# Weight blocks cast by DMAs that GpSimd issues, the scale applied to y instead of w_in, a written-out order for group 1, and four output buffers

## The chip, the cores and the metric

The kernel runs on one core of a Trainium2 chip. The metric is device time of one execution in microseconds, lower is better. A core has TensorE (PE, matmuls into PSUM), VectorE (DVE), ScalarE (ACT), GpSimd (POOL) and SyncE (SP), each with a queue of its own that it works through in order, and 16 DMA engines that all queues share. DMAs are issued by SP (the profile calls their queue q1, hardware_dynamic) or by POOL (q0, software_dynamic).

## The reference

Two parts, the first feeding the second. Shapes: q, k, v and f_logit are (4, 8, 768, 48), w_in is 384 x 2048, w_out is 2048 x 384, all float32.

```python
f = 1.0 / (1.0 + np.exp(-f_logit))
for t in range(S):                                   # per batch and head, state is 48 x 48
    state = f[:, :, t, :, None] * state + np.einsum('bhd,bhe->bhde', k[:, :, t], v[:, :, t])
    y[:, :, t] = np.einsum('bhd,bhde->bhe', q[:, :, t], state)
x = y.transpose(0, 2, 1, 3).reshape(B * S, H * D)    # 3072 x 384
h = x @ w_in
P = a[0] + a[1] * h + a[2] * h**2 + a[3] * h**3
Q = 1.0 + np.abs(b[0]) * np.abs(h) + np.abs(b[1]) * h**2
out = (P / (Q + 1e-06)) @ w_out
```

## The kernel before

**Tiling.** The sequence is cut in 6 chunks of 128 positions. In the recurrent part a unit n is one chunk for two of the four batches, so there are 12 units; in the dense part a group n is one chunk (all four batches, 512 rows) and 512 of the 2048 hidden columns, so there are 24 groups, four to a chunk. Unit 2c and 2c+1 give the input xT of chunk c, which groups 4c to 4c+3 read.

**A unit** is built by functions named a_: `a_ef` (ACT, two activations of the forget logits fn, L110 and L111), `a_cs` (PE, cumulative sum, L117), `a_exp` twice (ACT, tiles A, L124), `a_mul` (DVE, qn and kn times A into qkp, L130 and L131), `a_T` and `a_Te` (PE transposes L139, ACT evacuation L147), `a_sc` twice (PE scores, L181), `a_mask` twice (DVE, scm, L190), `a_sv`, `a_al`, `a_st` (the state: PE, ACT, DVE L234), `a_y` and `a_ye` (PE L201, ACT evacuation ysb L217), `a_x` and `a_xe` (PE transposes L242, ACT xT L250).

**A group** is built by functions named m_: `m_h` twice (PE, half a group each, L263), `m_y` (ACT, hy, L271), `m_sq` and `m_abs` (DVE, h2 shown as h L277, z L282), `m_p1` (DVE, tile t, L326 and L327), `m_p2` (pb, L332), `m_p3` (L336), `m_u` and `m_ln` twice (PE L291, ACT lq L313), `m_ex` (ACT qi, L320), `m_g` (DVE gall, L343). `m_o` and `m_oe` are the output product (PE L360) and its evacuation to osb with a DMA to HBM (ACT L368 or DVE L366, SP L369); they run for the chunk before.

**Order.** The pools are rings, but the order of the instructions on each engine is that of the source (`manual_schedule`). A prologue from L383 to L515 takes units 0 to 2 and groups 0 and 1 as far as L336; `busy(k)` in it are k matmuls on zeros. Then one loop over n takes group n further together with the unit that is due, with a branch for odd and one for even n, and conditions for n == 1. A last part handles chunk 5 without units.

**Loads.** `load(n)` issues two DMAs each for fn, kn and qn on SP (192 KB each, in pieces of 192 bytes) and two for vn on POOL, which cast float32 to bfloat16 on the way; the ld pool holds three units. Weights come in eight blocks of 768 KB: `load_w_in(g)` and `load_w_out(g)` issue a DMA on SP into one of two float32 staging buffers (wst), and POOL casts the block to bfloat16. For w_in POOL also multiplies by `sig[:, 0:1]`, one number that depends on b alone (`coefficients()` computes it), because the dense part works on a scaled h. Group g of chunk 0 needs block g of w_in; the w_out blocks are first read by `m_o` in iteration n = 5.

**Output tail.** The last chunk's four products use three PSUM tiles: b = 0 and 1 share the tile `op2`, b = 2 has `opl`, b = 3 has `op`. osb has two buffers (pool ms).

## Time and profile before

| | us |
|---|---|
| median of 3 runs | 285.42 |
| the 3 runs | 284.39, 285.42, 287.75 |
| profiled execution | 285.07 |
| its span, first to last instruction | 283.2 |
| its mean granted TensorE clock | 0.958 |

The profiled execution lies 0.35 us under the median, and 1.87 us of its time lie outside the span. In the profile's rows the first number is the start and the second the duration in us; brackets at the end of a row tell how long the engine sat idle before it and what ended the wait. A row of several instructions has their count as x2.

### The profile page before, as it was taken

How to read it: one execution, taken by the hardware profiler on the slowest of the kernel's cores; microseconds unless marked ns; L12 is line 12 of the kernel's file. 1: busy time of each engine (PE TensorE's matmuls, PEld its weight loads, DVE VectorE, ACT ScalarE, POOL GpSimd, SP SyncE). 2: the span in 40 equal slices, each digit the busy share in tenths (PEclk: the TensorE clock that was granted, in tenths of full speed). 3: DMA queues.
4: the chain of work that ended last, by engine and by line, in shares of the span. 5: the costliest groups of instructions: out<-in, count | busy, mean ns of one | idle time of the engine just before them, and what ended most of it. 6: DMA issues, size and time to landing. Idle time of an engine off the chain costs nothing.

```text
span 283.2 us, 4853 instructions
## 1 busy us (share of the span) xinstructions
PE 237.9 (84%) x1992; PEld 127.5 (45%) x1992; DVE 236.8 (84%) x249; ACT 226.0 (80%) x235; POOL 51.9 (18%) x42
## 2 busy tenths in 40 slices
PE   7589762668678799899898998998998979999982
PEld 2255322343343365455554545554555444445541
DVE  4265199975999999998999989999989997799931
ACT  3275560857999999999999999999999976897920
POOL 7008699907020200200202002000000000000000
PEclk9979996869999799999999999999999999999997
DMA  9999989999970320890942914909300000001003
GB/s 130 172 241 184 196 202 256 185 249 206 177 66 0 19 11 30 123 129 2 160 92 51 172 33 87 136 30 165 59 27 3 28 30 28 17 11 58 29 28 111
DMA packets 107317, 27.83 MB, mean 98 GB/s; under 512 B 100640, under 2 KB 105760, under 8 KB 107296
## 3 DMA queue, kind: packets, MB, share of 16 engines
q1 hardware_dynamic: 82336, 25.18, 42.9%
q0 software_dynamic: 24960, 2.36, 15.8%
q8 instruction: 15, 0.25, 0.4%
q14 instruction: 6, 0.05, 0.1%
HBM read 25.17 MB, written 4.72 MB: 106 GB/s over the span
## 4 chain that ended last, share of the span: by engine, by line
PE 37%; DVE 21%; ACT 17%; issue 9%; SPq 8%; DMA 5%; POOL 1%; ACTq 0%; DVEq 0%
PE hp L263 14%; PE op L360 12%; SPq L101 8%; PE u L291 7%; ACT hy L271 4%; ACT lq L313 4%; DVE h L277 3%; DVE t L327 3%; DMA wst<-in_moe_w_in_dram 2%; DVE t L326 2%; ACT A L124 2%; DMA fn<-in_f_logit_dram 2%; PE tp L139 2%; DVE pb L332 2%; DVE t L336 2%
## 5 line engine op out<-in xcount | busy, mean ns | idle before, releaser
L263 PE MATMUL hp<-xT,w_in_sb 128*128 128x512 bf16 x288 | 67.1, 382 | 7.3 <-ACT xT L250 4.0
L360 PE MATMUL op<-w_out_sb,gall 128*128 128x384 bf16 x368 | 63.8, 326 | 1.4 <-DVE gall L343 0.8
L313 ACT ACTIVATE lq<-u,sig 128x1024 f32<-128x1024 f32 x44 | 47.8, 1125 | 5.4 <-PE u L291 4.5
L271 ACT CAST hy<-hp 128x1024 bf16<-128x1024 f32 x48 | 47.5, 1007 | 5.1 <-PE hp L263 4.5
L360 PEld LDWEIGHTS <-gall 128*128 128x128 bf16 x384 | 36.9, 98 | 27.7 <-DVE gall L343 1.2
L320 ACT ACTIVATE qi<-lq 128x2048 bf16<-128x2048 f32 x24 | 46.0, 1916 | 0.2
L263 PEld LDWEIGHTS <-w_in_sb 128*128 128x128 bf16 x288 | 27.5, 98 | 39.0 <-issue 8.4
L277 DVE TENSOR_TENSOR h<-hy 128x2048 bf16<-128x2048 bf16 x24 | 29.7, 1239 | 14.6 <-ACT hy L271 14.5
L101 POOL DMA_DIRECT2D vn<-in_v_dram x24 | 22.7, 951 | 94.8 <-PE y L201 94.0
L190 DVE TENSOR_TENSOR scm<-sc,mask 128x1024 bf16<-128x1024 f32 x24 | 29.0, 1218 | 7.1 <-PE sc L181 6.9
L327 DVE TENSOR_TENSOR t<-t,h 128x2048 bf16<-128x2048 bf16 x24 | 33.5, 1396 | 0.8
L291 PE MATMUL u<-h,dg 128*128 128x512 bf16 x88 | 27.4, 394 | 6.1 <-ACT A L124 5.6
L343 DVE TENSOR_TENSOR gall<-t,qi 128x2048 bf16<-128x2048 bf16 x24 | 29.2, 1218 | 2.1 <-ACT qi L320 2.1
L147 ACT COPY qkT<-tp 128x2048 bf16<-128x2048 bf16 x12 | 22.5, 1877 | 10.6 <-PE tp L139 10.6
L336 DVE TENSOR_TENSOR t<-t,pb 128x2048 bf16<-128x2048 bf16 x24 | 29.3, 1220 | 0.5
L291 PEld LDWEIGHTS <-dg 128*128 128x128 bf16 x176 | 16.9, 100 | 26.7 <-issue 11.6
L291 PE MATMUL u<-z,dg 128*128 128x512 bf16 x88 | 27.4, 395 | 0.0
L139 PE MATMUL tp<-ident,qkp 128*128 128x128 bf16 x192 | 16.0, 242 | 11.3 <-DVE qkp L130 9.9
L326 DVE TENSOR_SCALAR t<-hy,a_sb 128x2048 bf16<-128x2048 bf16 x24 | 24.5, 1021 | 0.0
L375 POOL TENSOR_SCALAR w_in_sb<-wst,sig 128x1536 bf16<-128x1536 f32 x4 | 19.1, 4773 | 18.3 <-DMA wst<-in_moe_w_in_dram 18.3
L124 ACT ACTIVATE A<-cs 128x768 f32<-128x768 f32 x24 | 19.3, 818 | 1.7 <-PE cs L117 1.7
L332 DVE TENSOR_SCALAR pb<-hy,a_sb 128x2048 bf16<-128x2048 bf16 x24 | 19.8, 824 | 0.0
(59 smaller groups left out, 236.7 us busy)
## 6 DMA issues: line engine op xcount, KB each, us to landing
fn<-in_f_logit_dram SPq DMA_DIRECT2D x24, 192.0 KB, 5.0
kn<-in_k_dram SPq DMA_DIRECT2D x24, 192.0 KB, 5.5
qn<-in_q_dram SPq DMA_DIRECT2D x24, 192.0 KB, 5.0
out_dram<-osb SPq DMA_DIRECT2D x24, 192.0 KB, 1.9
wst<-in_moe_w_in_dram SPq DMA_DIRECT2D x4, 768.0 KB, 6.5
wst<-in_moe_w_out_dram SPq DMA_DIRECT2D x4, 768.0 KB, 7.4
vn<-in_v_dram POOLq DMA_DIRECT2D x24, 96.0 KB, 5.4
b_sb<-in_moe_b_dram SPq DMA_DIRECT2D x1, 1.0 KB, 5.4
```

Source lines behind the costliest of these rows:

```text
L101: eng.dma_start(out=dst[:, j], in_=src[u * UB + j, :, t0:t0 + C, :].rearrange("h t d -> t h d"))
L263: nc.tensor.matmul(hp[:, e, :], w_in_sb[:, kk, m * P:(m + 1) * P], xT[:, kk, :], start=(kk == 0), stop=(kk == KD - 1))
L271: nc.scalar.copy(s["y"][:, half * 2 * NT:(half + 1) * 2 * NT], s["hp", half].rearrange("p a n -> p (a n)"))
L277: nc.vector.tensor_mul(s["h2"], s["y"], s["y"])
L291: nc.tensor.matmul(u[:, e, :], dg[:, 1 - i, :], src[:, (half * 2 + e) * NT:(half * 2 + e + 1) * NT], start=(i == 0), stop=(i == 1))
L313: nc.scalar.activation(s["lq"][:, half * 2 * NT:(half + 1) * 2 * NT], s["u", half].rearrange("p a n -> p (a n)"), AF.Ln, scale=sig[:, 2:3] ...
L320: nc.scalar.activation(s["qi"], s["lq"], AF.Exp, scale=-1.0)
L326: nc.vector.tensor_scalar(s["t"], s["y"], a_sb[:, 3:4], a_sb[:, 2:3], op0=ALU.mult, op1=ALU.add)
L327: nc.vector.tensor_mul(s["t"], s["t"], s["h2"])
L336: nc.vector.tensor_add(s["t"], s["t"], s["pb"])
L343: nc.vector.tensor_mul(galls[c][:, g * G:(g + 1) * G, :].rearrange("p a n -> p (a n)"), s["t"], s["qi"])
L360: nc.tensor.matmul(ops[c, b], galls[c][:, mm, b * C:(b + 1) * C], w_out_sb[:, mm, :], start=(mm == 0), stop=(mm == KF - 1))
```

## The change

`load_w_in` takes two of the blocks (0 and 1) over the staging buffers as before, but POOL's cast no longer multiplies, and both DMAs go out ahead of `load(2)`. Blocks 2 and 3 of w_in and all four of w_out are moved by one DMA each that POOL issues and that casts on the way; they write the bfloat16 weights directly. The factor `sig[:, 0:1]` is applied when ACT evacuates y (`a_ye`). The iteration n = 1 has its instructions written out in an order of their own. osb gets four buffers, and the last four outputs are handled in the order b = 2, 0, 1, 3 with three copies on DVE and one on ACT.

```diff
     def a_ye(n):
...
-        nc.scalar.copy(ysb.rearrange("t b (p i e) -> t i (b p) e", p=HP, i=2),
-                       s["y"].rearrange("t i b p e -> t i (b p) e"))
+        nc.scalar.activation(ysb.rearrange("t b (p i e) -> t i (b p) e", p=HP, i=2),
+                             s["y"].rearrange("t i b p e -> t i (b p) e"), AF.Copy, scale=sig[:, 0:1])
...
-        osb = ms.tile([P, DM], F32, name="osb")
+        osb = ms.tile([P, DM], F32, name="osb", bufs=4)
...
-    def load_w_in(g):
-        t = wst.tile([P, KD, G * P], F32, name="wst")
-        nc.sync.dma_start(out=t, in_=moe_w_in[:, g * G * P:(g + 1) * G * P].rearrange("(ko ki) n -> ki ko n", ki=P))
-        nc.gpsimd.tensor_scalar(w_in_sb[:, :, g * G * P:(g + 1) * G * P], t, sig[:, 0:1], None, op0=ALU.mult)
+    def load_w_in(g, dma_cast=True):
+        cols = slice(g * G * P, (g + 1) * G * P)
+        src = moe_w_in[:, cols].rearrange("(ko ki) n -> ki ko n", ki=P)
+        if dma_cast:
+            nc.gpsimd.dma_start(out=w_in_sb[:, :, cols], in_=src)
+        else:
+            t = wst.tile([P, KD, G * P], F32, name="wst")
+            nc.sync.dma_start(out=t, in_=src)
+            return lambda: nc.gpsimd.tensor_copy(w_in_sb[:, :, cols], t)
 
     def load_w_out(g):
-        t = wst.tile([P, G, DM], F32, name="wst")
-        nc.sync.dma_start(out=t, in_=moe_w_out[g * G * P:(g + 1) * G * P, :].rearrange("(ko ki) n -> ki ko n", ki=P))
-        nc.gpsimd.tensor_copy(w_out_sb[:, g * G:(g + 1) * G, :], t)
+        nc.gpsimd.dma_start(out=w_out_sb[:, g * G:(g + 1) * G, :],
+                            in_=moe_w_out[g * G * P:(g + 1) * G * P, :].rearrange("(ko ki) n -> ki ko n", ki=P))
...
-    load_w_in(0)
+    cast0 = load_w_in(0, False)
+    cast1 = load_w_in(1, False)
     load(2)
-    load_w_in(1)
+    cast0()
+    cast1()
+    load_w_in(2)
+    load_w_in(3)
...
-    load_w_in(2)
-    load_w_in(3)
     load(3)
...
-    load_w_out(0)
-    load_w_out(1)
     load(4)
+    for g in range(NG):
+        load_w_out(g)
...
     for n in range(1, NGR - NG):
+        if n == 1:
+
+            m_sq(1)
+            m_abs(1)
+            m_u(0, 0)
+            m_ln(0, 0)
+            a_sc(2, 0)
...
+            a_exp(3, 0)
+            a_exp(3, 1)
+            m_h(2, 0)
+            a_mask(2, 0)
+            a_sc(2, 1)
...
+            continue
...
-            if n == 2:
-                load_w_out(2)
-                load_w_out(3)
...
-    for b in range(B):
+    for b in (2, 0, 1, 3):
         m_o(NC - 1, b, range((NG - 1) * G, NG * G))
-        m_oe(NC - 1, b, (nc.scalar, nc.vector)[b % 2])
+        if b != 0:
+            m_oe(NC - 1, b, (nc.scalar, nc.vector)[b // 2])
+        if b == 1:
+            m_oe(NC - 1, 0, nc.vector)
```

The order on POOL, from the vn loads of unit 1 on, before (two vn rows are one unit's loads; L375 is the cast with the factor, L380 the cast of w_out):

```order
L101 DMA vn<-in_v_dram 128x8x48 x2
L375 TENSOR_SCALAR w_in_sb<-wst,sig 128x3x512
L101 DMA vn<-in_v_dram 128x8x48 x2
L375 TENSOR_SCALAR w_in_sb<-wst,sig 128x3x512 x3
L101 DMA vn<-in_v_dram 128x8x48 x2
L380 CAST w_out_sb<-wst 128x1536 x2
```

and after the change, at the same place (L380 is now the cast of w_in blocks 0 and 1):

```order
L101 DMA vn<-in_v_dram 128x8x48 x4
L380 CAST w_in_sb<-wst 128x3x512 x2
L376 DMA w_in_sb<-in_moe_w_in_dram 128x3x512 x2
L101 DMA vn<-in_v_dram 128x8x48 x4
L383 DMA w_out_sb<-in_moe_w_out_dram 128x4x384 x4
```

The vn loads of unit 2 move ahead of all casts, two casts are left of eight, and six weight DMAs stand on POOL, two ahead of the vn loads of units 3 and 4 and four behind them.

The order on SP, from the last load of unit 1 to the first of unit 3 (one piece of the difference; wst is the staging buffer):

```order
 L101 DMA qn<-in_q_dram 128x8x48 x2
-L374 DMA wst<-in_moe_w_in_dram 128x3x512
+L379 DMA wst<-in_moe_w_in_dram 128x3x512 x2
 L101 DMA fn<-in_f_logit_dram 128x8x48 x2
 L101 DMA kn<-in_k_dram 128x8x48 x2
 L101 DMA qn<-in_q_dram 128x8x48 x2
-L374 DMA wst<-in_moe_w_in_dram 128x3x512 x3
```

Block 1 moves ahead of the loads of unit 2, and the loads of unit 3 follow those of unit 2 with nothing between.

The order on DVE in iteration n = 1, from pb of group 1 to h2 of group 2, before (scm and state are unit 2's, qkp is unit 3's):

```order
L332 TENSOR_SCALAR pb<-hy,a_sb 128x2048
L190 TENSOR_TENSOR scm_656<-sc,mask 128x1024
L190 TENSOR_TENSOR scm_658<-sc,mask 128x1024
L234 TENSOR_TENSOR state_103<-sv,alast 128x384
L130 TENSOR_TENSOR qkp_100<-qn,A_640 128x2x8x48
L131 TENSOR_TENSOR qkp_100<-kn,A_695 128x2x8x48
L336 TENSOR_TENSOR t<-t,pb 128x2048
L343 TENSOR_TENSOR gall<-t,qi 128x2048
L277 TENSOR_TENSOR h_750<-hy 128x2048
```

and after:

```order
L190 TENSOR_TENSOR scm_648<-sc,mask 128x1024
L332 TENSOR_SCALAR pb<-hy,a_sb 128x2048
L190 TENSOR_TENSOR scm_673<-sc,mask 128x1024
L130 TENSOR_TENSOR qkp_100<-qn,A_637 128x2x8x48
L131 TENSOR_TENSOR qkp_100<-kn,A_639 128x2x8x48
L234 TENSOR_TENSOR state_103<-sv,alast 128x384
L336 TENSOR_TENSOR t<-t,pb 128x2048
L343 TENSOR_TENSOR gall<-t,qi 128x2048
L277 TENSOR_TENSOR h_744<-hy 128x2048
```

The same nine instructions; one scm moves ahead of pb, and state behind the two products of unit 3. On ACT the two exponentials of unit 3, qi and the two hy of group 2 now stand ahead of ysb of unit 2, which stood between those exponentials before.

More of the change, by code (lines that the diff above doesn't have):

```diff
@@ L512 @@
     m_p3(0)
-    load_w_out(0)
-    load_w_out(1)
     load(4)
+    for g in range(NG):
+        load_w_out(g)
     for n in range(1, NGR - NG):
+        if n == 1:
[4 more added lines that the diff above has]
+            a_sc(2, 0)
+            m_u(0, 1)
+            m_ln(0, 1)
+            a_sv(2)
+            a_al(2)
+            m_p1(1)
+            a_cs(3)
+            a_exp(3, 0)
[3 more added lines that the diff above has]
+            a_sc(2, 1)
+            m_p2(1)
+            m_h(2, 1)
+            m_ex(0)
+            m_y(2, 0)
+            m_y(2, 1)
+            a_mask(2, 1)
+            a_y(2)
+            a_ye(2)
+            a_mul(3)
+            a_st(2)
+            a_x(2)
+            a_xe(2)
+            a_T(3)
+            a_Te(3)
+            m_p3(1)
+            m_g(0)
+            continue
         gp_, gn, gh = n - 1, n, n + 1
@@ L521 @@
             mu, mf = (n + 5) // 2, (n + 3) // 2
-            if isu(mu) and n > 1:
+            if isu(mu):
                 a_exp(mu, 0)
@@ L526 @@
                 m_abs(gn)
-            if n == 1:
-                m_u(gp_, 0)
-                m_ln(gp_, 0)
-                m_u(gp_, 1)
-                m_ln(gp_, 1)
-                a_sc(mf, 0)
-                a_sv(mf)
-                a_al(mf)
-                a_cs(mu)
-                a_exp(mu, 0)
-                a_sc(mf, 1, ring=True)
-                m_p1(gn)
-                m_p2(gn)
-                a_mask(mf, 0)
-                a_mask(mf, 1)
             if isu(mf):
@@ L546 @@
                 a_exp(mu, 1)
-            if isg(gp_) and n > 1:
+            if isg(gp_):
                 m_u(gp_, 0)
@@ L571 @@
             if isg(gn):
-                if n > 1:
-                    m_p1(gn)
-                    m_p2(gn)
+                m_p1(gn)
+                m_p2(gn)
                 m_p3(gn)
```

## The prediction

> **What bounds the kernel now.** I read the page first (busy shares, the slices), then the windows by stage, then the timeline of DVE, POOL, ACT and PE in the slow stage, then the DMA queues and the tail.
>
> ```profile
> PE 237.9 (84%) x1992; PEld 127.5 (45%) x1992; DVE 236.8 (84%) x249; ACT 226.0 (80%) x235; POOL 51.9 (18%) x42
> POOL 7008699907020200200202002000000000000000
> DMA  9999989999970320890942914909300000001003
> ```
>
> No engine is full on average. Each slice is 7.08 us: POOL and the DMAs work in the first ten and hardly afterwards. The windows (busy us per engine, then clock, DMA share, GB/s) say the same of DVE and ACT:
>
> ```profile
> core 0: us, PE busy (x) PEld busy (x) DVE busy (x) ACT busy (x) POOL busy (x), PEclk, DMA share, GB/s
> 31.50:50.00 18.50, 9.30 (x48) 4.57 (x48) 14.67 (x9) 7.20 (x9) 17.84 (x6) 0.85 1.02 207
> 50.00:68.00 18.00, 12.69 (x122) 7.22 (x121) 13.54 (x13) 12.34 (x14) 8.53 (x6) 0.77 1.26 210
> 106.00:240.00 134.00, 125.22 (x1122) 68.09 (x1121) 126.10 (x132) 127.22 (x136) 6.99 (x8) 1.00 0.45 72
> ```
>
> From 106 to 240 us three engines are busy 93 to 95% of the time: that stage is tight, and the change leaves its order alone. From 31.5 to 68 ACT is busy 19.5 of 36.5 us; something holds it. DVE in that stage:
>
> ```profile
> 35.30 1.23 DVE L277 TENSOR_TENSOR h<-hy 128x2048 bf16<-128x2048 bf16 x1 [6.14 <-ACT hy L271]
> 37.04 4.57 DVE L326 TENSOR_SCALAR t<-hy,a_sb 128x2048 bf16<-128x2048 bf16 x1
> 41.65 4.18 DVE L327 TENSOR_TENSOR t<-t,h 128x2048 bf16<-128x2048 bf16 x1
> 46.48 0.95 DVE L130 TENSOR_TENSOR qkp<-qn,A 128x768 bf16<-128x768 f32 x1
> 51.09 1.95 DVE L326 TENSOR_SCALAR t<-hy,a_sb 128x2048 bf16<-128x2048 bf16 x1
> 53.07 2.37 DVE L327 TENSOR_TENSOR t<-t,h 128x2048 bf16<-128x2048 bf16 x1
> 56.52 2.33 DVE L190 TENSOR_TENSOR scm<-sc,mask 128x1024 bf16<-128x1024 f32 x2
> 60.99 0.96 DVE L131 TENSOR_TENSOR qkp<-kn,A 128x768 bf16<-128x768 f32 x1 [0.81 <-ACT A L124]
> 63.80 1.23 DVE L343 TENSOR_TENSOR gall<-t,qi 128x2048 bf16<-128x2048 bf16 x1 [0.72 <-ACT qi L320]
> 67.92 1.63 DVE L277 TENSOR_TENSOR h<-hy 128x2048 bf16<-128x2048 bf16 x1 [2.90 <-ACT hy L271]
> ...
> L327 DVE TENSOR_TENSOR t<-t,h 128x2048 bf16<-128x2048 bf16 x16 | 19.6, 1225 | 0.6
> L326 DVE TENSOR_SCALAR t<-hy,a_sb 128x2048 bf16<-128x2048 bf16 x16 | 12.9, 806 | 0.0
> ...
> 31.48 14.16 POOL L375 TENSOR_SCALAR w_in_sb<-wst,sig 128x1536 bf16<-128x1536 f32 x3 [2.66 <-DMA wst<-in_moe_w_in_dram]
> 48.60 5.77 POOL L380 CAST w_out_sb<-wst 128x1536 bf16<-128x1536 f32 x2 [0.66 <-DMA wst<-in_moe_w_out_dram]
> ```
>
> In the tight stage L326 takes 0.81 us and L327 1.23 (the two rows with means, window 100 to 240). Beside POOL's casts they take 4.57 and 4.18, later 1.95 and 2.37. So DVE is held 3.76 + 2.95 = 6.7 us, then 1.14 + 1.14 = 2.3 us. Behind the first two stands the product of unit 2 (L130, 46.48), for which PE and ACT wait. This is the bound of the stage.
>
> **The change, part by part.** The sum is made against the profiled execution (285.07 us, span 283.2).
>
> *Casts off POOL.* Six casts go, and the two left read blocks 0 and 1, which now land one behind the other.
>
> ```profile
> 22.09 4.93 POOL L375 TENSOR_SCALAR w_in_sb<-wst,sig 128x1536 bf16<-128x1536 f32 x1 [15.62 <-DMA wst<-in_moe_w_in_dram]
> 65.02 1.47 POOL L380 CAST w_out_sb<-wst 128x1536 bf16<-128x1536 f32 x1 [8.94 <-DMA wst<-in_moe_w_out_dram]
> ```
>
> A plain cast takes 1.47 us alone. Block 0 came at 22.09; with 1.5 us of delay (below) and some 3 us for block 1 behind it both casts start by 27, and at 1.5 to 4.9 us each they end before the first h2 (35.30 + 1.5). So the holds of 6.7 and 2.3 us go. From the h2 of group 0 (35.30) to that of group 2 (67.92) DVE takes 32.6 us: 9.0 held, 0.81 + 0.72 + 2.90 = 4.4 idle, and 19.2 its own work.
>
> *Order of n = 1.* What is late next? Count from the product of unit 2, L130.
>
> ```profile
> 49.85 1.87 ACT L147 COPY qkT<-tp 128x2048 bf16<-128x2048 bf16 x1 [9.09 <-PE tp L139]
> 53.24 2.10 ACT L313 ACTIVATE lq<-u,sig 128x1024 f32<-128x1024 f32 x2
> ```
>
> ACT evacuates qkT 3.4 us after L130, then the logits of unit 3, and ends the two lq 8.9 us after it (55.34 - 46.48). In the new order half of `m_h(2)` follows on PE when lq frees its PSUM buffer, then the second scores, at about 1.5 and 0.5 us; only then can DVE do the second scm, 10.9 us after L130. Its own work up to there takes 56.52 - 46.48 = 10.0, less 2.3 held, plus one scm (half of 2.33): 8.9. So it now waits 2.0 us at that place. The three idle stretches of 4.4 us go: A, qi and hy of group 2 come ahead of ysb on ACT, each with over 1 us to spare by the same count. From h2 to h2 that makes 19.2 + 2.0 = 21.2 us instead of 32.6: **-11.4 us**. Bounds: -9.0 if the reordering gains nothing, -13.4 if the new wait is absent too. I take -11.4, the count.
>
> *vn of unit 2 earlier.* Its two DMAs now go on POOL's queue right behind those of unit 1 (4.70 + 1.78, so near 6.5 us), while unit 1's logits are awaited.
>
> ```profile
> q0 software_dynamic: 1156, 0.11, 206.6%
> q1 hardware_dynamic: 169, 0.03, 27.6%
> ...
> q1 hardware_dynamic: 1832, 0.33, 121.2%
> ...
> q0 software_dynamic: 24960, 2.36, 15.8%
> ...
> 4.70 1.78 POOL L101 DMA_DIRECT2D vn<-in_v_dram  x2
> ...
> 14.87 0.84 ACT L110 ACTIVATE ef<-fn 128x768 f32<-128x768 f32 x1 [5.54 <-DMA fn<-in_f_logit_dram]
> 16.49 1.85 ACT L147 COPY qkT<-tp 128x2048 bf16<-128x2048 bf16 x1
> ```
>
> The first two rows are the packets of the stretch 8.5 to 9.5 us: with vn queued the SP loads fall to 169 packets in 1 us, and they have 916 per us when vn is through (third row, 11 to 13 us). 24960 packets on 24 vn DMAs are 1040 each, so two more take 2080 / 1156 = 1.8 us, in which SP's loads lose 82%: 1.5 us. ACT waits for fn of unit 1 (14.87), and the first evacuation (16.49) stands right behind it, with the chain to the first group after that. **+1.5 us**; bounds 0 and 1.8. The Trainium skill (DMA: Bandwidth & Descriptors, "Queues, rings and completion order") has each DMA engine alternate between its queues; with 1325 packets per us shared evenly the loss would be 0.9 us, and the sum 0.6 us lower. The rows of 8.5 to 9.5 us do not show an even share, so I keep 1.5.
>
> *Weight DMAs that cast.* The trace has no cast of rows this long.
>
> ```profile
> DMA packets 286, 0.56 MB, mean 279 GB/s; under 512 B 14, under 2 KB 14, under 8 KB 286
> ```
>
> That is SP's uncast weight traffic in 28 to 30 us. Six blocks are 4.72 MB: 16.9 us at 279 GB/s. By vn's rate (1156 packets of 192 read bytes per us, 222 GB/s) 21 us. If vn's packets ran one at a time (15.8% of 283.2 us x 16 engines / 24960 = 28.7 ns, 107 GB/s) 44 us. I take 17 to 21: share 206.6% shows that they overlap. Block 2 is needed when lq is done, near 50 us, and block 3 about 10 us later; POOL issues them near 30. w_out has until n = 5, over 90 us. The loads of unit 3 now follow those of unit 2 on SP without the staging waits, but share with the weights: 6144 rows at 916 per us are 6.7 us, beside 17 to 21 us of weights and 4160 / 1156 = 3.6 us of vn from about 30. At an even share they land by 47, with SP starved as at 8.5 to 9.5 by 56; the product of unit 3 wants them at 35.3 + 1.5 + (46.48 - 35.30 - 6.7) + 10.9 + 1.2 = 53.4. **+0.5 us**; bounds 0 and 22 (the 44 us price, rival below).
>
> *Scale on y.* Rows with means, from the lines of ACT:
>
> ```profile
> L320 ACT ACTIVATE qi<-lq 128x2048 bf16<-128x2048 f32 x24 | 46.0, 1916 | 0.2
> L217 ACT CAST ysb<-y 128x768 bf16<-128x768 f32 x12 | 9.6, 800 | 6.0 <-PE y L201 6.0
> L307 ACT ACTIVATE lq<-w,sig 128x2048 f32<-128x2048 bf16 x2 | 4.0, 2010 | 0.0
> ```
>
> An activation with its scale in a tile (L307) takes 0.09 us more than one without at 2048 elements, 0.03 at 768: 12 x 0.03 = **+0.4 us**, all counted as on the path; bounds 0 and 1.1 (12 x 0.09).
>
> *Tail.*
>
> ```profile
> 272.36 2.76 PE L360 MATMUL op<-w_out_sb,gall 128*128 128x384 bf16 x16
> 275.69 0.81 PE L360 MATMUL op<-w_out_sb,gall 128*128 128x384 bf16 x4 [0.57 <-ACT osb L368]
> 277.62 0.48 ACT L368 COPY osb<-opl 128x384 f32<-128x384 f32 x1 [1.99 <-DMA out_dram<-osb]
> 279.15 0.56 DVE L366 COPY osb<-op 128x384 f32<-128x384 f32 x1 [2.00 <-DMA out_dram<-osb]
> ```
>
> Copies wait for a free osb, which four buffers end, and PE waits 0.57 for a copy of the tile that b = 0 and 1 share, which the new order ends. Then 28 matmuls run from 272.36 at 0.17 us and end near 277.2; the last copy follows at 277.3 to 277.6 behind two others on DVE, instead of 279.15. **-1.7 us**; bounds 0 (the last DMAs queue behind each other) and -2.
>
> *Sum:* -11.4 + 1.5 + 0.5 + 0.4 - 1.7 = -10.7. The 1.87 us outside the span stay. 285.07 - 10.7 = 274.4, and 0.35 more to stand for the median: 274.7, rounded to **275 us**.
>
> **Rivals.**
>
> *The weights crowd out the loads of unit 3.* POOL's queue takes the DMA engines as at 8.5 to 9.5 us, and at 21 us for the weights plus landing time qn of unit 3 arrives near 59. Then DVE's in-order queue stands 6 us: 281. For it: the 169 packets. Against it: POOL comes to the weights near 30 us, when SP's loads of unit 3 can be on their way, and an even share lands them by 47.
>
> *The casting DMA is slow: slower than before.* If long rows go at 107 GB/s, 44 + 3.6 us from 30 make qn of unit 3 land near 76, 23 us after it is wanted: 275 + 23 = 298. It becomes slower than before once qn lands 10.7 us late, at 64, which needs about 30 us for the six blocks (157 GB/s). For it: 29 ns a vn packet. Against it: the overlap.
>
> *DVE and POOL's DMA issues hold each other.* The h2 row at 67.92 took 1.63 beside two issues, 0.4 more than the 1.23 at 35.30. Ten issues ahead of the steady stage at 0.4 each on DVE: +4, 279. Against it: two weight issues and most vn issues fall ahead of 36.8, where DVE idles 6.14 us. The Trainium skill (SBUF — State Buffer, "SBUF: two separate sides") says that GpSimd cannot write descriptors while DVE runs in a mode that takes both ports; by that rule the w_out blocks come late, which are needed last. What that costs here no run shows yet.
>
> *The gain is given back.* The stage after 68 us follows something that the change doesn't move, so that only tail and slip count: 285.07 + 1.5 + 0.4 - 1.7 = 285. Against it: in 106 to 240 us ACT is busy 127.2 of 134, and DMA only 0.45.
>
> **How the numbers follow.** Forecast 275: 0.66 (own range 272 to 278). Crowding, 281: 0.14. Mutual holds, 279: 0.08. Given back, 285: 0.05. Slow cast, 298: 0.07. A measurement of this kernel tells about 1% from no change, 2.9 us. Under 282.6 lie the forecast, the holds and half or more of the crowding: faster 0.82. Within 1%: the rest of the crowding and the giving back, 0.11. Slower 0.07. The range reaches from 271.5 (the order gains its 13.4 and the slip is small) to 283, past the crowding; what is left out is the 0.12 of the last two and some of the crowding.
>
> **What would show it.** Right: L326 and L327 of groups 0 and 1 at 0.8 and 1.2 us; the third h2 near 58 instead of 67.92; ef of unit 1 near 16.4; DVE waiting for PE about 2 us ahead of the second scm of unit 2; no wait for a DMA at any osb. Wrong: L130 of unit 3 or `m_h(2)` waiting for a DMA; L217 over 0.9 us; the windows after 106 us longer than before.

## The result and the profile after

| | before | after |
|---|---|---|
| median, runs | 284.90, 4 runs | 275.42, 4 runs |
| shortest to longest run | 284.16 to 287.75 | 275.34 to 275.86 |
| profiled execution, its span | 285.07, 283.2 | 275.51, 273.7 |
| mean granted TensorE clock | 0.958 | 0.984 |

The ratio of the times is 0.965 (95% interval 0.958 to 0.972): 9.5 us faster. The forecast was 275.

First the page of the changed kernel: the busy shares, and POOL in 40 slices of 6.84 us.

```profile
PE 231.2 (84%) x1961; PEld 124.8 (46%) x1992; DVE 228.6 (84%) x250; ACT 226.2 (83%) x234; POOL 30.9 (11%) x42
POOL 8105740020202002002002002000000000000000
```

POOL's busy time falls from 51.9 to 30.9 us, and what is left of it at 34 us and later are DMA issues. The windows by stage (length, then busy us of PE, PEld, DVE, ACT and POOL, then clock, DMA share, GB/s):

```profile
36.00:46.00 10.00, 7.25 (x44) 3.41 (x43) 7.68 (x9) 7.39 (x9) 1.03 (x2) 1.00 1.57 153
46.00:58.00 12.00, 7.09 (x97) 3.81 (x97) 9.06 (x11) 10.84 (x12) 1.76 (x2) 1.00 1.21 179
58.00:70.00 12.00, 9.25 (x118) 5.18 (x118) 11.96 (x13) 11.59 (x13) 0.47 (x1) 1.00 1.34 189
97.00:231.00 134.00, 123.67 (x1101) 67.93 (x1118) 125.63 (x131) 127.81 (x135) 7.00 (x8) 1.00 0.44 72
```

The two slow stretches of before (36.5 us, ACT busy for 19.5 of them) have become 22 us with ACT busy for 18.2, and from 58 us on DVE and ACT are full. The tight stage is nearly as it was. DVE's timeline from the start to the third h2, with POOL's cast and ACT's ef of unit 1 ahead of it:

```profile
16.47 0.84 ACT L110 ACTIVATE ef<-fn 128x768 f32<-128x768 f32 x1 [7.35 <-DMA fn<-in_f_logit_dram]
...
23.28 1.78 POOL L380 CAST w_in_sb<-wst 128x1536 bf16<-128x1536 f32 x1 [15.07 <-DMA wst<-in_moe_w_in_dram]
...
22.78 0.95 DVE L130 TENSOR_TENSOR qkp<-qn,A 128x768 bf16<-128x768 f32 x1
23.65 2.22 DVE L131 TENSOR_TENSOR qkp<-kn,A 128x768 bf16<-128x768 f32 x1
...
38.28 1.23 DVE L277 TENSOR_TENSOR h<-hy 128x2048 bf16<-128x2048 bf16 x1 [6.25 <-ACT hy L271]
...
40.03 0.81 DVE L326 TENSOR_SCALAR t<-hy,a_sb 128x2048 bf16<-128x2048 bf16 x1
40.87 1.22 DVE L327 TENSOR_TENSOR t<-t,h 128x2048 bf16<-128x2048 bf16 x1
...
52.86 1.23 DVE L190 TENSOR_TENSOR scm<-sc,mask 128x1024 bf16<-128x1024 f32 x1 [1.59 <-PE sc L181]
55.40 0.96 DVE L130 TENSOR_TENSOR qkp<-qn,A 128x768 bf16<-128x768 f32 x1 [1.31 <-DMA qn<-in_q_dram]
...
59.88 1.22 DVE L277 TENSOR_TENSOR h<-hy 128x2048 bf16<-128x2048 bf16 x1
```

The holds of L326 and L327 (4.57 and 4.18 before) are gone, and from the first h2 to the third DVE takes 21.60 us instead of 32.62. Three things cost: the first h2 comes at 38.28 instead of 35.30, DVE waits 1.59 us for the second scores, and 1.31 us for q of unit 3. At 23.65 the product of unit 1 takes 2.22 us instead of 0.95 while POOL casts.

Where the span's 9.5 us went can be read off the starts of the h2 alone, of which every group has one. Rows of this kind carry all comparisons below (us):

| stretch | before | after | difference |
|---|---|---|---|
| start to first h2 | 35.30 | 38.28 | +2.98 |
| first to third h2 | 32.62 | 21.60 | -11.02 |
| third to fourth | 9.65 | 8.98 | -0.67 |
| fourth to 11th | 65.64 | 66.16 | +0.52 |
| 11th to 21st | 93.91 | 94.29 | +0.38 |
| 21st to 24th (last) | 24.19 | 24.18 | -0.01 |
| last h2 to end of span | 21.89 | 20.21 | -1.68 |

### The profile page after: what moved, and what is told of

Its sections match the earlier page's. It is cut to its first block, busy times and chain, and to the rows that moved or that the text cites. A ratio compares the mean times of both kernels' runs of the same rounds, so it can differ in the third digit from the quotient of the medians.

```text
span 273.7 us, 4806 instructions
## 1 busy us (share of the span) xinstructions
PE 231.2 (84%) x1961; PEld 124.8 (46%) x1992; DVE 228.6 (84%) x250; ACT 226.2 (83%) x234; POOL 30.9 (11%) x42
## 3 DMA queue, kind: packets, MB, share of 16 engines
q0 software_dynamic: 27872, 4.72, 21.8%
## 4 chain that ended last, share of the span: by engine, by line
PE 42%; ACT 19%; DVE 16%; DMA 8%; issue 7%; SPq 6%; DVEq 0%; ACTq 0%
PE hp L263 15%; PE op L360 14%; PE u L291 7%; SPq L101 6%; DMA qn<-in_q_dram 6%; ACT A L124 4%; ACT lq L313 3%; ACT hy L271 3%; DMA fn<-in_f_logit_dram 3%; ACT qkT L147 2%; ACT ysb L217 2%; DVE gall L343 2%; DVE h L277 2%; DVE t L327 2%; DVE t L336 2%
## 5 line engine op out<-in xcount | busy, mean ns | idle before, releaser
L263 PE MATMUL hp<-xT,w_in_sb 128*128 128x512 bf16 x277 | 65.7, 379 | 6.6 <-ACT xT L250 4.0
L263 PEld LDWEIGHTS <-w_in_sb 128*128 128x128 bf16 x288 | 27.2, 98 | 37.0 <-issue 7.7
L101 POOL DMA_DIRECT2D vn<-in_v_dram x24 | 21.4, 898 | 121.0 <-PE y L201 120.2
L327 DVE TENSOR_TENSOR t<-t,h 128x2048 bf16<-128x2048 bf16 x24 | 29.4, 1225 | 0.8
L291 PE MATMUL u<-h,dg 128*128 128x512 bf16 x71 | 22.9, 385 | 6.9 <-ACT A L124 6.6
L291 PE MATMUL u<-z,dg 128*128 128x512 bf16 x88 | 27.1, 390 | 1.0 <-issue 0.2
L130 DVE TENSOR_TENSOR qkp<-qn,A 128x768 bf16<-128x768 f32 x12 | 11.4, 950 | 10.6 <-DMA qn<-in_q_dram 10.6
L139 PE MATMUL tp<-ident,qkp 128*128 128x128 bf16 x192 | 13.9, 224 | 7.2 <-DVE qkp L130 4.7
L326 DVE TENSOR_SCALAR t<-hy,a_sb 128x2048 bf16<-128x2048 bf16 x24 | 19.4, 808 | 0.0
L332 DVE TENSOR_SCALAR pb<-hy,a_sb 128x2048 bf16<-128x2048 bf16 x24 | 19.4, 807 | 0.0
```

The source lines that it names most:

```text
L101: eng.dma_start(out=dst[:, j], in_=src[u * UB + j, :, t0:t0 + C, :].rearrange("h t d -> t h d"))
L263: nc.tensor.matmul(hp[:, e, :], w_in_sb[:, kk, m * P:(m + 1) * P], xT[:, kk, :], start=(kk == 0), stop=(kk == KD - 1))
L291: nc.tensor.matmul(u[:, e, :], dg[:, 1 - i, :], src[:, (half * 2 + e) * NT:(half * 2 + e + 1) * NT], start=(i == 0), stop=(i == 1))
L327: nc.vector.tensor_mul(s["t"], s["t"], s["h2"])
```

## The experiments

Each is the changed kernel with one edit unless said otherwise. In e1 and e10 the edit adds eight lines near the top, so that L138 is the L130 of the others, and so on. "Before" ran beside them each time: its median was 285.70 beside e1 to e4, 285.22 beside the repeated changed kernel and e5 to e7, 285.02 beside e8, e10 and e12, and 285.21 beside e13. Medians of different groups are therefore comparable to about half a microsecond.

| run | median (runs) | ratio to before | first h2 | first to third | third to fourth |
|---|---|---|---|---|---|
| changed kernel again | 276.01 (6) | 0.968 [0.965, 0.971] | 39.34 | 21.70 | 8.99 |
| e1 | 276.19 (4) | 0.965 [0.957, 0.972] | 36.48 | 22.71 | 9.69 |
| e2 | 275.35 (4) | 0.963 [0.957, 0.970] | 39.22 | 21.20 | 8.98 |
| e3 | 276.33 (4) | 0.967 [0.959, 0.975] | 37.84 | 21.74 | 8.98 |
| e4 | 277.93 (4) | 0.972 [0.967, 0.977] | 38.14 | 22.29 | 9.29 |
| e5 | 280.21 (4) | 0.983 [0.979, 0.987] | 38.80 | 24.20 | 9.15 |
| e6 | 275.79 (6) | 0.967 [0.964, 0.970] | 39.27 | 20.19 | 9.89 |
| e7 | 280.66 (4) | 0.984 [0.981, 0.988] | 35.24 | 27.89 | 11.26 |
| e8 | 276.51 (4) | 0.971 [0.966, 0.976] | 36.65 | 22.70 | 11.93 |
| e10 | 274.37 (6) | 0.964 [0.960, 0.969] | 36.63 | 20.20 | 10.08 |
| e12 | 275.20 (6) | 0.954 [0.948, 0.961], its three shortest | 39.01 | 20.67 | 9.89 |
| e13 | 271.37 (6) | 0.952 [0.949, 0.956] | 34.66 | 20.18 | 9.25 |

**The changed kernel again.**

> The changed kernel unaltered, as the yardstick for the runs beside it. Theory (the stage is set by fixed waits): 275.4 as at first, third h2 21.6 us after the first, the product of unit 3 waiting about 1.3 us for its q. Rival (chance of the clock): the dip of the granted clock at 14 to 22 us (0.71 and 0.86 in the first trace) lies elsewhere or is deeper, and the third h2 moves by up to 1 us with it; then differences under 1 us between single profiles mean nothing and medians have to be compared.

The rival holds for the start. The h2 rows move by 1 us with nothing changed. In this profile the clock of 18 to 26 us is lower, and PE starts the scores of unit 1 1.05 us later (29.83 against 28.78), though DVE's products for them end only 0.1 us later. The windows of the first profile, then of this one:

```profile
18.00:26.00 8.00, 5.50 (x75) 3.17 (x76) 5.49 (x5) 4.43 (x6) 2.34 (x2) 0.93 1.04 276
```
```profile
18.00:26.00 8.00, 6.29 (x66) 3.58 (x67) 5.38 (x5) 4.33 (x6) 2.38 (x2) 0.50 1.05 278
```

So a first h2 is known to 1 us from one profile. "First to third" agrees to 0.1 here (21.60, 21.70), but not always: e4, whose edit lies in the tail alone, has 22.29, with DVE idle for 2.02 us ahead of the product of unit 3. In the three runs without that idle time (e6, e10, e13) the stretch repeats to 0.02.

**e1: v of unit 2 behind POOL's casts.**

```diff
-    load(2)
+    load(2, late_v=True)
     cast0()
     cast1()
+    load_v(2)
     load_w_in(2)
```

`late_v` leaves the two DMAs of v out of the load, and `load_v` issues them.

> The changed kernel with the two vn DMAs of unit 2 put on POOL behind the two casts instead of right behind those of unit 1. Theory (the vn packets delay fn of unit 1, which ACT waits for): ef of unit 1 starts near 14.9 us instead of 16.47, the vn packets end near 11 us instead of 14, and the time falls by 1.3 to 1.6 us, to about 274.0. The product L131 of unit 1 may still be held by the first cast. Rival (the first evacuation waits for something else, such as the two weight blocks now ahead of the loads of unit 2): ef of unit 1 stays near 16.4 and the time within 0.4 us of 275.4.

ACT's ef of unit 1 and DVE's product of unit 3 here:

```profile
14.68 0.84 ACT L118 ACTIVATE ef<-fn 128x768 f32<-128x768 f32 x1 [5.36 <-DMA fn<-in_f_logit_dram]
...
54.71 0.96 DVE L138 TENSOR_TENSOR qkp<-qn,A 128x768 bf16<-128x768 f32 x1 [1.96 <-DMA qn<-in_q_dram]
```

The slip was v's: ef is back at 14.68 (16.47 with v early) and the first h2 comes 1.8 us sooner. The time did not follow. q of unit 3 lands when the DMA queues let it, so its wait grew from 1.31 to 1.96 us; the wait for the second scores grew from 1.59 to 2.06, and third to fourth h2 took 0.7 longer. At the fourth h2 nothing was left of the gain (68.88 against 68.86).

**e2: the two casts behind the product of unit 1.**

```diff
     load(2)
-    cast0()
-    cast1()
-    load_w_in(2)
-    load_w_in(3)
...
     a_mul(1)
+    hold = consts.tile([C, 1], BF16, name="hold")
+    nc.gpsimd.tensor_copy(hold, at_[1]["qk"][:, 0, 1, 0, 0:1])
+    cast0()
+    cast1()
+    load_w_in(2)
+    load_w_in(3)
```

The copy of one column makes POOL wait for the product.

> The changed kernel with the two casts of w_in put behind the product of unit 1: POOL first copies one element of that product, so that it waits for L131. Theory (the cast that starts at 23.28 holds L131 of unit 1, 2.22 us instead of 0.95, and everything up to the first group comes later by that): L131 takes 0.95, the first h2 starts near 37.0 instead of 38.28, and the time falls by 1.0 to 1.3 us, to about 274.2. Rival (L131 is long because its data come late, or the delay is hidden later): L131 stays above 2 us, or the first h2 comes earlier and the time stays within 0.4 us of 275.4.

DVE's product of unit 1 and the next scm, and the window of that stretch:

```profile
23.93 0.95 DVE L131 TENSOR_TENSOR qkp<-kn,A 128x768 bf16<-128x768 f32 x1
...
30.16 2.36 DVE L190 TENSOR_TENSOR scm<-sc,mask 128x1024 bf16<-128x1024 f32 x2 [4.80 <-PE sc L181]
```
```profile
18.00:26.00 8.00, 6.14 (x66) 3.55 (x66) 4.56 (x5) 4.50 (x6) 1.05 (x2) 0.50 1.01 284
```

The mechanism is shown: without the cast beside it, L131 takes 0.95. Its worth is not. With the clock at 0.50, PE was still at its matmuls on zeros when the product was done, and began the transposes that follow it only at 26.65; the scores started at 29.72 instead of 28.78, DVE's wait grew from 2.88 to 4.80, and the first h2 fell at 39.22. The median (275.35) can't be told from the changed kernel's.

Two other runs give the price. e8, below, casts plainly on POOL too, but has ef of unit 1 at 14.84, as before (14.87), and the clock at 0.98 from 18 to 26 us; only L131 is held:

```profile
22.02 2.22 DVE L131 TENSOR_TENSOR qkp<-kn,A 128x768 bf16<-128x768 f32 x1
```

Its first h2 comes at 36.65, 1.35 us after that of before. And e6, whose edit acts only after the start, has both products held (2.12 and 2.23 us) and its first h2 at 39.27 with the clock at 1.00.

**e3: plain copy at the y evacuation.** The factor is left out of the computation.

```diff
-        nc.scalar.activation(ysb.rearrange("t b (p i e) -> t i (b p) e", p=HP, i=2),
-                             s["y"].rearrange("t i b p e -> t i (b p) e"), AF.Copy, scale=sig[:, 0:1])
+        nc.scalar.copy(ysb.rearrange("t b (p i e) -> t i (b p) e", p=HP, i=2),
+                       s["y"].rearrange("t i b p e -> t i (b p) e"))
```

> The changed kernel with the plain copy at the evacuation of y, so the factor on y is left out of the computation. Theory (each ysb costs 0.11 us more with the factor read from a tile, 0.908 instead of 0.800, and all of the steady stage passes through it): ysb back at 0.80, the time from the fourth to the last h2 shorter by about 0.9 us, time about 274.4. Rival (ACT has room for it): ysb 0.80 but the time within 0.3 us of 275.4.

ACT's groups, first of the changed kernel, then of e3:

```profile
L217 ACT ACTIVATE ysb<-y,sig 128x768 bf16<-128x768 f32 x12 | 10.9, 908 | 2.7 <-PE y L201 2.7
```
```profile
L217 ACT CAST ysb<-y 128x768 bf16<-128x768 f32 x12 | 9.6, 804 | 2.8 <-PE y L201 2.7
```

The factor costs 104 ns a time. From the 11th to the 21st h2 e3 takes 93.91 us, as before the change and as e7 (93.92), which copies too; the kernels with the factor take 94.26 to 94.30. So some 0.38 us of it are on the path there. From the 4th to the 11th h2 e3 takes 66.15 against 66.16: nothing. The median (276.33, runs over 4 us) could not show 0.4.

**e4: the old tail.**

```diff
-        osb = ms.tile([P, DM], F32, name="osb", bufs=4)
+        osb = ms.tile([P, DM], F32, name="osb")
...
-    for b in (2, 0, 1, 3):
+    for b in range(B):
         m_o(NC - 1, b, range((NG - 1) * G, NG * G))
-        if b != 0:
-            m_oe(NC - 1, b, (nc.scalar, nc.vector)[b // 2])
-        if b == 1:
-            m_oe(NC - 1, 0, nc.vector)
+        m_oe(NC - 1, b, (nc.scalar, nc.vector)[b % 2])
```

> The changed kernel with two osb buffers and the old order of the last four outputs. Theory (the tail gains 1.7 us by the waits for a free buffer): the last copies wait 2.0 us for a DMA again and the time rises by 1.5 to 1.9 us, to about 277.1. Rival (the last DMAs set the end either way): within 0.5 us of 275.4.

DVE's last copy:

```profile
272.18 0.56 DVE L366 COPY osb<-op 128x384 f32<-128x384 f32 x1 [2.00 <-DMA out_dram<-osb]
```

The wait of 2.00 us for a free osb is back, and from the last h2 to the end it takes 276.1 - 254.34 = 21.8 us, against 20.2 with the new tail and 21.9 before. The tail is worth 1.6 us by the rows. By the medians it is 1.9 (277.93 against 276.01), but these come from different groups.

**e5: the old order of n = 1**, weights cast by the DMA.

```diff
-        if n == 1:
+        if n == -1:
...
-            if isu(mu):
+            if isu(mu) and n > 1:
...
+            if n == 1:
+                m_u(gp_, 0)
+                m_ln(gp_, 0)
...
+                a_mask(mf, 1)
```

The written-out block is never entered; the one that comes back stands in the branch for odd n, as before.

> The changed kernel with the order of n = 1 as it was before; the weights still cast by the DMA. Theory (the prediction's split of the 11.4 us: 9.0 for the casts, 2.4 for the order): L326 and L327 of groups 0 and 1 stay at 0.81 and 1.22, the three idle stretches ahead of the product of unit 3, of gall and of the third h2 come back (together 4.4 us or somewhat more), the wait ahead of the second scm goes; first to third h2 23.6 to 24.2 us, time 277.4 to 278.0 (+2.0 to +2.6). Rival (the order is worth nothing, the casts are all): 275.4. Rival (the order is the main part and the DMA casts alone bring little): 280 or more.

DVE from the second scm to the third h2:

```profile
51.99 1.23 DVE L190 TENSOR_TENSOR scm<-sc,mask 128x1024 bf16<-128x1024 f32 x1 [0.20 <-PE sc L181]
...
55.10 0.96 DVE L130 TENSOR_TENSOR qkp<-qn,A 128x768 bf16<-128x768 f32 x1 [1.43 <-DMA qn<-in_q_dram]
...
63.00 1.23 DVE L277 TENSOR_TENSOR h<-hy 128x2048 bf16<-128x2048 bf16 x1 [3.51 <-ACT hy L271]
```

First to third h2 took 24.20, in the range expected. The largest idle time is back where it was: 3.51 us ahead of the third h2, for hy. ACT in turn waited 2.43 us for hp of PE, which in this order began its matmuls (L263) at 58.67, behind the transposes of unit 3, and in the changed kernel at 51.04, ahead of them: so this gap goes by PE's order at least as much as by ACT's. Another 1.43 us ahead of the product of unit 3 are a wait for its q. The profiled execution is 2.4 us longer than the changed kernel's beside it, the medians differ by 4.2; of its four runs (278.94 to 281.62) the profiled one was the shortest, so the rows show the smaller share. The median lies outside the expected 277.4 to 278.0, in the range of the second rival; which stretch takes the rest, no trace shows.

**e7: the old casts**, with the factor on POOL, in the new order and with the new tail; y is copied plainly and the loads stand in their old places.

```diff
-    cast0 = load_w_in(0, False)
-    cast1 = load_w_in(1, False)
+    load_w_in(0)
     load(2)
-    cast0()
-    cast1()
-    load_w_in(2)
-    load_w_in(3)
+    load_w_in(1)
...
     def load_w_in(g):
+        nc.gpsimd.tensor_scalar(w_in_sb[:, :, g * G * P:(g + 1) * G * P], t, sig[:, 0:1], None, op0=ALU.mult)
```

> The changed kernel with the weights of before: staged by SP, cast by POOL with the scale on w_in, plain copy at the y evacuation, loads in their old places; new order of n = 1 and new tail stay. Theory (the order takes away the three idle stretches of 4.4 us, the holds of 9.0 us stay and cover the new wait ahead of the second scm; no startup slip; tail -1.7 to -2.4): L326 and L327 of group 0 at 4 to 4.6 us again, first to third h2 28.0 to 28.8 us, time 278.3 to 279.3. Rival (the order helps only once the casts are gone, since DVE in its order behind the holds is the bound): first to third h2 32 us, time 282.6 to 283.4. Rival (the order is most of the gain): under 277.

DVE at group 0 and group 2, and POOL:

```profile
37.34 4.57 DVE L326 TENSOR_SCALAR t<-hy,a_sb 128x2048 bf16<-128x2048 bf16 x1
41.94 4.18 DVE L327 TENSOR_TENSOR t<-t,h 128x2048 bf16<-128x2048 bf16 x1
...
65.71 2.36 DVE L327 TENSOR_TENSOR t<-t,h 128x2048 bf16<-128x2048 bf16 x1
...
32.46 13.46 POOL L375 TENSOR_SCALAR w_in_sb<-wst,sig 128x1536 bf16<-128x1536 f32 x3 [3.79 <-DMA wst<-in_moe_w_in_dram]
```

The first two holds are those of before to the hundredth. First to third is 27.89, a little under the 28.0 to 28.8 expected; the time is 1.4 us above its range, and 1.6 us lie in the third to fourth h2 (11.26 against 9.65 before), where the last two w_out casts now hold L327 and L332 of group 2. With e5 this makes a square of first to third h2, in us:

| | old order | new order |
|---|---|---|
| casts on POOL | 32.62 | 27.89 |
| casts by DMA | 24.20 | 21.60 |

The casts alone give 8.4, the order alone 4.7, both together 11.0, each from single profiles.

**e8: plain casts on POOL** for all eight blocks; the factor stays at y. As e7, but:

```diff
-        nc.gpsimd.tensor_scalar(w_in_sb[:, :, g * G * P:(g + 1) * G * P], t, sig[:, 0:1], None, op0=ALU.mult)
+        nc.gpsimd.tensor_copy(w_in_sb[:, :, g * G * P:(g + 1) * G * P], t)
```

> The changed kernel with all eight weight blocks staged by SP and cast by POOL as before, but with a plain cast (the scale stays on the y evacuation); new order and tail stay. It asks what of the gain needs the casting DMA and what only a shorter POOL cast (1.5 to 2.2 us where the one with the scale took 4.2 to 4.9). Theory (a plain cast holds DVE for its own length wherever it meets DVE): no startup slip, first h2 at 35.2 to 36; holds at L326 and L327 of groups 0 and 1 of 2 to 5 us in sum instead of 9, first to third h2 23.5 to 26 us, second hold of some 2 us by the w_out casts after the third h2 as in the run with the old casts; time 276.5 to 279. Rival (the scale on POOL was all that cost): first to third h2 under 22 us, time 274 or less. Rival (any POOL cast costs the same): 280 or more.

DVE beside the casts:

```profile
37.80 1.96 DVE L282 TENSOR_SCALAR z<-hy 128x2048 uint16<-128x2048 uint16 x1
...
47.24 1.96 DVE L326 TENSOR_SCALAR t<-hy,a_sb 128x2048 bf16<-128x2048 bf16 x1
...
59.35 2.48 DVE L277 TENSOR_TENSOR h<-hy 128x2048 bf16<-128x2048 bf16 x1
```

Each cast that meets DVE holds it 1.2 to 1.3 us. First to third h2 is 22.70, under the range expected, third to fourth 11.93. Yet the median is 276.51, at the lower end of the range and 0.5 above the changed kernel's 276.01: of the 4.65 us between the medians of e7 and the changed kernel, 4.15 are had by taking the multiplication off POOL. As the change places them, the casting DMAs save nothing over plain casts that the runs (275.38 to 278.86) could tell. The profiled execution is the longest of the four, 2.4 us above the median, so its rows show the holds but not where the shorter ones get their time.

**e6: w_out DMAs at the end of n = 2.**

```diff
     load(4)
-    for g in range(NG):
-        load_w_out(g)
...
             if isu(mu + 2) and n > 0:
                 load(mu + 2)
+            if n == 2:
+                for g in range(NG):
+                    load_w_out(g)
```

> The changed kernel with the four w_out DMAs issued at the end of n = 2, behind the load of unit 5, instead of ahead of the loop; blocks then land from about 70 us on and are needed from 90 us. Theory (the w_out blocks share the DMA engines row for row with the loads of unit 3, so its q lands late): in 46 to 52 us POOL's queue carries no weight packets, q of unit 3 lands about 4 us earlier (51 instead of 55), the wait of 1.31 us at the product of unit 3 goes, and the third h2 comes 1.0 to 1.3 us earlier; time 274.1 to 274.4. Rival (what is gained is lost again because the product then waits for A of unit 3 on ACT): the product moves by less than 0.5 us and the time stays at 275.4. Rival (w_out then lands too late for the first m_o): PE waits for a DMA at L360 near 90 us, 277 or more.

The DMA queues from 46 to 52 us (packets, MB written, share of the time), first in the changed kernel, then in e6, and e6's product of unit 3 on DVE:

```profile
q0 software_dynamic: 1183, 0.88, 93.8%
q1 hardware_dynamic: 1182, 0.22, 33.9%
```
```profile
q1 hardware_dynamic: 6300, 1.19, 123.1%
```
```profile
54.99 0.95 DVE L130 TENSOR_TENSOR qkp<-qn,A 128x768 bf16<-128x768 f32 x1
```

With w_out queued, SP's loads get one packet for each of POOL's: 1182 in 6 us, against 6300 without. In e6 the product of unit 3 waits for nothing and the third h2 comes 1.4 us earlier after the first. But third to fourth h2 took 9.89 instead of 8.98: `z` took 0.96 beside the w_out DMA issues that now fall there (0.69 otherwise), and DVE waited 0.42 for scores of PE, whose clock was 0.60 in 58 to 62 us. The median gained 0.2. (One execution of e6 took 586.72 us; the ratio leaves it out, the median of the other five is 275.63, and nothing here explains it.)

**e10: e1 and e6 together.**

> Two edits together that each moved their own wait and left the time where it was: v of unit 2 behind POOL's first casts, and the w_out DMAs at the end of n = 2. Theory (each alone only uncovered the other: the earlier start ran into the late q of unit 3, and the earlier q came behind the late start): ef of unit 1 at 14.7, first h2 at 36.5, no DMA wait at the product of unit 3, first to third h2 20.2 us, third h2 near 56.7 where it was 59.9 and 61.0; time 272.6 to 273.6. Rival (what is gained up to the third h2 goes again, because the clock then dips or PE is late in the stage from the third to the fourth h2, 9.9 us instead of 9.0): 273.8 to 274.6. Rival (something after 70 us sets the pace whatever comes ahead): 275.5 to 276.

Third and fourth h2:

```profile
56.83 1.22 DVE L285 TENSOR_TENSOR h<-hy 128x2048 bf16<-128x2048 bf16 x1
...
66.91 1.23 DVE L285 TENSOR_TENSOR h<-hy 128x2048 bf16<-128x2048 bf16 x1 [0.26 <-ACT hy L279]
```

Up to the third h2 both gains add as the theory has it (56.83 against 59.88 and 61.04). Then 1.1 us go again from the third to the fourth, as the first rival has it, with its time (274.37); as in e6, `z` took 0.97 and DVE waited 0.40 for scores. Against the changed kernel's 276.01 that is -1.6 us, with intervals of the ratio that overlap a little.

**e12: no cast on POOL at all**, the weights starting when the product of unit 0 is done.

```diff
-    cast0 = load_w_in(0, False)
-    cast1 = load_w_in(1, False)
+    hold = consts.tile([C, 1], BF16, name="hold")
+    nc.gpsimd.tensor_copy(hold, at_[0]["qk"][:, 0, 1, 0, 0:1])
+    load_w_in(0)
+    load_w_in(1)
     load(2)
-    cast0()
-    cast1()
     load_w_in(2)
     load_w_in(3)
```

with w_out as in e6.

> All eight weight blocks by the casting DMA, so that POOL casts nothing: blocks 0 and 1 issued on POOL's queue when the first product of unit 0 is done (POOL waits on it with a copy of one column), v of unit 2 behind them, then blocks 2 and 3; w_out at the end of n = 2. It asks whether POOL's two casts at 22 to 27 us hold the products of unit 1, and what the casting DMA costs when it comes still earlier. Theory (the casts hold L130 or L131 by 1.3 us, more when both are met): L130 and L131 of unit 1 take 0.95 each, ef of unit 1 at 14.7, first h2 at 35.3 to 36.2, time 271.8 to 273.2. Rival (the queues share the DMA engines, so the weights now take the bandwidth from k and q of unit 1): the product of unit 1 waits for a DMA by 1 us or more, first h2 at 37 to 39, time 274 to 276. Rival (block 0 lands too late): PE waits for a DMA at L263 near 31 us.

DVE's product of unit 1:

```profile
24.76 0.96 DVE L130 TENSOR_TENSOR qkp<-qn,A 128x768 bf16<-128x768 f32 x1 [3.62 <-DMA qn<-in_q_dram]
25.64 0.95 DVE L131 TENSOR_TENSOR qkp<-kn,A 128x768 bf16<-128x768 f32 x1
```

Here the first rival holds: with the weights issued at 13.8 us, DVE waits 3.62 us for q of unit 1. The six runs lie between 270.75 and 277.35 (median 275.20), wider than any other kernel's but for e6's one outlier. The profiled execution took 276.30 and is one of the three longest; the three shortest (270.75, 271.41 and 274.10) left no trace, so whether they have this wait is not known. Two of them are as short as those of e13.

**e13: the same, started when q of unit 1 has landed.**

```diff
-    nc.gpsimd.tensor_copy(hold, at_[0]["qk"][:, 0, 1, 0, 0:1])
+    nc.gpsimd.tensor_copy(hold, at_[1]["qn"][:, 1, H - 1, 0:1])
```

> As the run without any POOL cast, but POOL waits for the q of unit 1 instead of the first product, so that the weights of blocks 0 and 1 start near 18 to 19 us, when the loads of unit 1 are through; v of unit 2, blocks 2 and 3 behind them, w_out at the end of n = 2. Theory (the weights held up q of unit 1 by their share of the DMA engines, and without that only the gain from the missing POOL casts is left): no DMA wait at the product of unit 1, L130 and L131 of unit 1 at 0.95 each, first h2 at 35.2 to 35.6 against 36.6 with the casts on POOL, first to third h2 20.2 us, time 272.6 to 273.6 with single runs no more than 3 us apart. Rival (blocks 0 and 1 now land too late, since the loads of unit 2 share the engines with them): PE waits for a DMA at L263 between 31 and 36 us, time 274.5 or more. Rival (the spread of the run before is of the clock and not of the DMA): runs again 5 us or more apart.

POOL's wait, the product of unit 1 and the first h2:

```profile
17.81 0.19 POOL L451 CAST hold<-qn 128x1 bf16<-128x1 f32 x1 [11.36 <-DMA qn<-in_q_dram]
...
20.42 0.95 DVE L130 TENSOR_TENSOR qkp<-qn,A 128x768 bf16<-128x768 f32 x1
21.29 0.95 DVE L131 TENSOR_TENSOR qkp<-kn,A 128x768 bf16<-128x768 f32 x1
...
34.66 1.22 DVE L277 TENSOR_TENSOR h<-hy 128x2048 bf16<-128x2048 bf16 x1 [6.25 <-ACT hy L271]
```

271.37 us, six runs within 1.3 us, 4.6 below the changed kernel and 1.2 below the range expected. Neither the DMA wait nor the hold is there, ef of unit 1 starts at 13.90 (14.87 before), and the first h2 comes at 34.66, ahead even of the 35.30 of before. With the start behind q the spread of e12 is gone too; that it came from the collision at unit 1 fits both, but is not shown. Against e10 (274.37), where blocks 0 and 1 still come over the staging buffers and POOL's casts, e13 is 3.0 us shorter; by the profiles 1.97 us of it are there at the first h2.

## Why the prediction was right, and where not

**The sum.** -10.7 was forecast against the profiled execution and -9.6 came (285.07 to 275.51); of the 1.1 us between, the 0.35 to the median and the rounding up to 275 had covered about half. The large terms held, and errors of about 1 us each stand among the small ones. That they nearly cancel is luck: the start cost 1.5 us more than forecast and the fourth to 11th h2 0.5 more, while DVE's stretch to the third h2 was 0.9 us shorter than counted apart from the wait for q, and the third to fourth gave 0.67 that no term had.

**The signs.** Those for "right" came: L326 and L327 at 0.81 and 1.22, ef of unit 1 at 16.47, the new wait at the second scm (1.59), and the third h2 at 59.88, a little later than "near 58". Those for "wrong" came too, each small: L130 of unit 3 waited for a DMA (1.31), L217 took 0.908, and the 11th to 21st h2 took 0.38 longer.

**Casts and order, -11.4.** Measured -11.0 for first to third h2, the wait for q, which belongs to the term of the weight DMAs, included. The split, 9.0 for the casts and 2.4 for the order on top, is 8.4 and 2.6 in the square. Within it two errors cancel: e6 shows that the stretch takes 20.2 us when q is in time, not the 21.2 that were counted (the new wait at the second scm is 1.59, not 2.0, and DVE's own work 18.6, not 19.2), and the wait for q added 1.3 to 1.4. What the term needs is the multiplication off POOL more than the casts: with plain casts there, e8 takes 22.70 where e7 takes 27.89.

**v of unit 2 earlier, +1.5.** Measured +1.60 at ef of unit 1, and e1 takes it away. Here the Trainium skill (DMA: Bandwidth & Descriptors, "Queues, rings and completion order") had queues served in turn, worth 0.9 instead of 1.5. The rows go both ways: from 46 to 52 us its rule holds to the packet (1183 to 1182), but from 8 to 10 us, with v queued, they were:

```profile
q0 software_dynamic: 2138, 0.20, 191.1%
q1 hardware_dynamic: 483, 0.09, 35.6%
```

Keeping the trace's share was right at this place. Why the two places differ stays open.

**The step that failed: the startup.** The prediction let the two casts left on POOL end "before the first h2" and concluded that they hold nobody. They meet the product of unit 1 at 22 to 26 us, which stands on the same path: L131 took 2.22 instead of 0.95, +1.27. With the +1.60 that is 2.87 of the slip of 2.98, of which 1.5 was forecast. e8 has this hold alone and slips by 1.35. In e13, which has neither these casts nor v of unit 2 ahead of the weights, the slip of the start is gone altogether.

**Casting weight DMAs, +0.5.** Measured 1.31 us of wait for q of unit 3 (1.42 in the second profile). The mechanism is the crowding rival's, at a quarter of its size. The 1183 packets of 46 to 52 us, 1536 bytes read each, are 303 GB/s, so the slow cast (157 GB/s and less) is excluded. Yet the six blocks were not through in 17 to 21 us. The first was issued at 27.1, and those of w_out, issued from 34.0 on, landed 13.3 to 19.2 us later, with the v loads of units 3 and 4 in the same queue. So q came near 55.4, close to the 56 that the prediction had for a starved SP, and not by 47. What was underrated is that an even share is one of packets: SP gets one short packet for each long one of POOL's. The profiled execution of e12, with the weights at the wrong time, shows a wait of this kind of 3.62 us.

**Factor on y, +0.4.** Each costs 0.10, not the 0.03 scaled down from 2048 elements: the 0.09 read there does not shrink with the size. Of the twelve only some lie on the path, 0.38 us in all by e3. The sum was right, its two factors were not, so the agreement is luck. The +0.52 from the 4th to the 11th h2 is not the factor's, since e3 has it too; its cause is open.

**Tail, -1.7.** Measured -1.68; e4 takes 1.6 of it back.

**Not foreseen.** The third to fourth h2 is 0.67 shorter, and not by the clock, which was 1.00 there in both kernels (68 to 78 us before, 59 to 69 after). In the rows of before, the third h2 took 1.63 us and the L326 behind it 1.05, against 1.22 and 0.81 after, 0.65 in sum:

```profile
67.02 1.47 POOL L380 CAST w_out_sb<-wst 128x1536 bf16<-128x1536 f32 x1 [0.53 <-DMA wst<-in_moe_w_out_dram]
...
70.08 1.05 DVE L326 TENSOR_SCALAR t<-hy,a_sb 128x2048 bf16<-128x2048 bf16 x1
```

The last w_out cast ran until 68.49, beside the first half microsecond of the h2 at 67.92. The prediction put that h2's extra 0.4 us down to the two issues that began at 68.43; the cast fits better, since the h2 at 68.86 after the change took 1.22 with two issues beside it from 69.53. The holding of DVE by POOL's DMA issues, a rival at +4, is small: it shows in `z` at 0.91 to 0.97 instead of 0.69 us, once or twice in a trace, and in that L326. The issues themselves were not held: the four of w_out took 3.00 us while DVE was idle (34.04) and 2.99 in e13 while it worked (53.43).

## What to carry to other kernels

An engine that shares a resource with the bottleneck has to be checked against every instruction of the path it overlaps, from the first one on, and not only at the place where it used to hurt. Bulk transfers that one queue issues take turns with the small rows of another, so give them a start (a wait on the load that must come first) and not only a place in an order: moving that one start took the runs from between 270.75 and 277.35 us (e12) to between 271.00 and 272.33 (e13). A wait taken away alone may show nothing (e1, e6): try the pair before the mechanism is dismissed.
